# Partial sums of two token blocks kept in HBM between groups, in a chain of retention, gated MLP and MLP

## The chip, the cores and the metric

The kernel runs on one core of one Trainium2 chip. The metric is the device time of one execution in microseconds (us); a time given for the kernel is the median of several executions. A profile comes from one further execution. Engines are named as the profile names them: PE (TensorE's matmuls), PEld (its weight loads), DVE (VectorE), ACT (ScalarE), POOL (GpSimd), SP (SyncE, which issues most transfers).

## The reference, cut to what matters

```python
# q, k, v: (2, 8, 768, 64); 8 heads with decay gamma
for t in range(S):
    state = gamma * state + k_t (outer) v_t
    y[t] = scale * q_t @ state
x = y as (1536 tokens, 512)
# gated MLP, d_ff 1536
xn = x / sqrt(mean(x*x) + 1e-6) * rms_g
x = (silu(xn @ w_gate) * (xn @ w_val)) @ w_out
# MLP, d_ff 2048
h = x @ w_in
out = maximum(0.01 * h, h) @ w_out2
```

Inputs and outputs are 32-bit floats. This document is about the two output products, `@ w_out` (layer 1, called `o` in the code) and `@ w_out2` (layer 2, `p`), and about where their partial sums over d_ff are kept.

## The kernel before

**Tiling.** The 1536 tokens are three blocks of 512 (b = 0, 1, 2). d_ff is cut into slices f of 128: 12 in layer 1, 16 in layer 2. Four slices make a group: gi = 0, 1, 2 belong to layer 1 and gi = 3, 4, 5, 6 to layer 2. The weights come as 64-bit numbers; per slice ScalarE (`prepare`, L537 and L538, tiles `wa` and `wb`) and VectorE make 32-bit numbers of the loaded `raw` tile, and then split them into a high and a low part (`w_...`, H on ScalarE, L on VectorE). A product of two split operands is three matmuls of 512 columns.

**Seven products.** Blocks 1 and 2 go through a scheme with seven products of halves in place of eight (`quad` for the products into the hidden layer, `seventh` for the output products of groups 1, 3, 4, 5 and 6). In `seventh` the products run in the order 1, 2, 5, 6, 3, 7, 4, with twelve matmuls each in a group (two pairs of slices, two banks, three terms). Products 1, 6, 7 and 4 add up in the two PSUM banks `X`, products 2, 5 and 3 in two banks `Z`. After each product but the first the two banks are, as they then stand, the contribution of this group to one half of one block: 2 to block 1 row 0, 5 and 7 to block 2 row 1, 6 and 3 to block 2 row 0, 4 to block 1 row 1. So twelve banks are read out per group. Product 7 goes on adding into the banks that product 6 left, and product 4 into those that product 7 left. The order of the products with whole blocks between them stands in `plan`: one block of twelve matmuls follows products 1, 2, 6 and 4.

**Where the sums live.** Block 1's and block 2's sums are two SBUF tiles of 128 x 4 x 512 (`x2acc` in layer 1, `y2acc` in layer 2, both in the places `acc1` and `acc2`). In group 0 ScalarE copies the banks there (`evac1`, L673). Later VectorE adds each bank to its part of the tile: in groups 1 and 3 to 6 in `seventh` (L817; the first contribution of a half in group 3 is a ScalarE copy, L815), in group 2 in `evac1` (L675). Block 0 has long been treated otherwise: ScalarE copies its banks to the tile `more`, and GpSimd's transfers write or add them to HBM (`held`, L695 to L698, in layer 1; the rows of `out`, L851 and L853, in layer 2).

**Queues.** Each engine executes in the order of its own queue. What stands in that order comes from the program's order (the string `ORDER` for the head of the program, `plan` and the rules of `run` with its costs for the rest) and from the framework's scheduler, which may move instructions of one engine past each other. Read-outs are put into `later` with the letter of their engine, "a" or "v", and come out with `flush` behind the step. `gh` and `gl` are pools of three buffers for the split hidden values (`gq_4h`, `gp_0h` and so on).

Of the kernel before, what the change touches and what calls it, by code (L numbers as in the profile page):

```python
# [8 lines left out]
F32 = mybir.dt.float32  # L9
# [7 lines left out]
P = 128  # L17
# [46 lines left out]
def chain_kernel(ctx: ExitStack, tc: tile.TileContext, qk_t, kv, w1, w2, mask, qdec, kdec, sdec, rms_g, ident, out):  # L64
# [26 lines left out]
    sm = attn_pools.enter_context(tc.tile_pool(name="sm", bufs=4))  # L91

    held = [dram.tile([P, 512], F32, name=f"held{i}") for i in range(4)]
    mask_sb = const.tile([P, 2, NPAIR, CH], F32, name="mask_sb")
    qdec_sb = const.tile([P, NPAIR, CH], F32, name="qdec_sb")
    kdecs = const.tile([P, CPB - 1, 2 * NPAIR, 1], F32, name="kdecs")
# [500 lines left out]
    def accumulate(L, g, f, b, start, stop, transposed):  # L597

        if start:
            acc["b"] = acc_banks(f"a{L}_{g}_{b}", 4)  # L600
        h, l = parted.pop((L, f, b))
        w = wt[f"{L}{f}"]
        for m in range(4):
            part = slice(m * P, (m + 1) * P)
            if transposed:
                terms = (w[:, 0, part], h), (w[:, 0, part], l), (w[:, 1, part], h)
            else:
                terms = (h[:, part], w[:, 0, :]), (h[:, part], w[:, 1, :]), (l[:, part], w[:, 0, :])
            cut = 256 if stop and m == 3 and g == len(groups) - 1 else 512
            for c in range(0, 512, cut):  # L610
                for n, (lhs, rhs) in enumerate(terms):
                    nc.tensor.matmul(  # L612
                        out=acc["b"][m][:, c:c + cut],
                        lhsT=lhs,
                        rhs=rhs[:, c:c + cut],
                        start=(start and n == 0),
                        stop=(stop and n == 2),
                        skip_group_check=True,
                    )
# [45 lines left out]
    def evac1(gi, b, banks):  # L665
        last = gi == len(G1) - 1
        if b:
            if gi == 0:
                acc[b] = xp.tile([P, 4, 512], F32, tag=f"acc{b}", name=f"x2acc{b}")
            for m in range(4):  # L670
                dst = acc[b][:, m, :]
                if gi == 0:
                    nc.scalar.activation(out=dst, in_=banks[m], func=AF.Copy)  # L673
                else:
                    nc.vector.tensor_tensor(out=dst, in0=banks[m], in1=dst, op=ALU.add)  # L675
            if not last:
                return
            highs, lows = ([lambda m=m, do=do: do(m) for m in range(2 * b - 2, 4)] for do in x2_parts(b))
            if b == 1:
                sums.extend(highs + lows)  # L680
                return
            one, two = slice(0, 2), slice(2, 4)
            ops = sums_of(acc, x2h, x2l, acc[1][:, one], acc[1][:, two], x2h[2][:, one], x2l[2][:, one], extra()[:, two])
            both = [lambda i=i: [ops[n]() for n in (f"{i}", f"h{i}")] for i in range(4)]
            sums.extend(both[:2] + [ops["l1"]] + highs + [ops["l0"]] + lows + [both[2], ops["l2"], both[3], ops["l3"]])
            return
        acc[0] = extra()
        for m in range(4):
            t = acc[0][:, m, :]
            if last:  # L690
                nc.vector.tensor_tensor(out=t, in0=banks[m], in1=t, op=ALU.add)
                continue
            nc.scalar.activation(out=t, in_=banks[m], func=AF.Copy)
            if gi == 0:
                nc.gpsimd.dma_start(out=held[m], in_=t)  # L695
            else:
                nc.gpsimd.dma_start(out=held[m], in_=t, accum_op=ALU.add)
                nc.gpsimd.dma_start(out=t, in_=held[m])  # L698
        if last:
            high, low = x2_parts(0)  # L700
            sums.extend([lambda m=m, do=do: do(m) for do in (high, low) for m in range(4)])

    def x2_parts(b):
        if b not in x2h:
# [27 lines left out]

    AS = {"o": "r", "p": "q"}
    turns = {}
    touched = set()

    def follow(q, f, n):
        t = turns[q, f]
# [17 lines left out]
    def seventh(gi, n, f):  # L756
        fs = groups[gi][1]
        L = groups[gi][0][-1]
        key = (AS[L], f, n)
        if n == 1 and f == fs[0]:  # L760
            gather(gi)
        if n == 5 and f == fs[0] and gi == len(groups) - 1:
            recall()
        upper(key)
        lower(key)
        h, l = parted.pop(key)
        unit, half, side, start, (b, row) = SIDES[n]
        names = f"{L}{f}", f"{L}{f + 1}", f"s{L}{f}", f"s{L}{f + 1}"
        w = wt[names[unit]]
        if f == fs[0] and start:  # L770
            acc[side] = [acc_bank(i + 2 * (side == "Z"), f"{side}{gi}_{n}_{i}") for i in range(2)]
        for m in range(2):
            part = slice((2 * half + m) * P, (2 * half + m + 1) * P)
            wh, wl = w[:, 0, part], w[:, 1, part]
            for k, (lhs, rhs) in enumerate(((wh, h), (wh, l), (wl, h))):
                nc.tensor.matmul(  # L776
                    out=acc[side][m],
                    lhsT=lhs,
                    rhs=rhs,
                    start=(start and f == fs[0] and k == 0),  # L780
                    stop=(f == fs[-2] and k == 2),
                    skip_group_check=True,
                )
        if n == 1:
            used(names[0])
        elif n == 4:
            used(names[1])
        elif n in (7, 3):
            free(names[unit])
        placed[0] = order.index(key) + 1  # L790
        if f != fs[-2]:
            return
        if n == 1:
            acc["Z"] = seeded = [acc_bank(i + 2, f"Z{gi}_2_{i}") for i in range(2)]
            source = acc["X"]

            def seed():
                for m in range(2):
                    nc.scalar.activation(out=seeded[m], in_=source[m], func=AF.Copy)

            later.append(("a", 1.2, seed))
            return
        banks = acc[side]
        total = y2 if L == "p" else acc
        fresh = gi == len(G1) and (b, row) not in touched
        if L == "p":
            touched.add((b, row))
        if b not in total:
            y2[b] = xp.tile([P, 4, 512], F32, tag=f"acc{b}", name=f"y2acc{b}")

        def put():
            for m in range(2):
                dst = total[b][:, 2 * row + m, :]
                if fresh:
                    nc.scalar.activation(out=dst, in_=banks[m], func=AF.Copy)  # L815
                else:
                    nc.vector.tensor_tensor(out=dst, in0=banks[m], in1=dst, op=ALU.add)  # L817
            if gi == len(groups) - 1 and LAST[b, row] == n:
                t = units.tile([P, 2, 16, 32], F32, tag="u", name=f"turned{b}_{row}")
                for m in range(2):  # L820
                    nc.vector.transpose(
                        out=t[:, m], in_=y2[b][:, 2 * row + m, :].rearrange("p (j r) -> p j r", r=32)
                    )
                    for i in range(4):
                        o = (2 * row + m) * P + i * 32
                        nc.sync.dma_start(
                            out=out[offs[b]:offs[b] + 512, o:o + 32].rearrange("(j r) d -> r j d", r=32),
                            in_=t[32 * i:32 * i + 32, m],
                        )

        later.append(("a" if fresh else "v", 1.2, put))

    def evac2(gi, b, banks):
        first, last = gi == len(G1), gi == len(groups) - 1
        if first and b:
            y2[b] = xp.tile([P, 4, 512], F32, tag=f"acc{b}", name=f"y2acc{b}")
        for m in range(4):
            dst = y2[b][:, m, :] if b else more[0][:, m, :]
            rows = out[offs[b] + m * P:offs[b] + (m + 1) * P, :]
            if b and not first:  # L840
                nc.vector.tensor_tensor(out=dst, in0=banks[m], in1=dst, op=ALU.add)
            elif last:
                cut = 256 if m == 3 else 512
                for c in range(0, 512, cut):
                    part = partial[m][:, c:c + cut]
# [1 line left out]
                    nc.sync.dma_start(out=rows[:, c:c + cut], in_=part)  # L847
            else:
                nc.scalar.activation(out=dst, in_=banks[m], func=AF.Copy)
                if not b and first:  # L850
                    nc.gpsimd.dma_start(out=rows, in_=dst)  # L851
                elif not b:
                    nc.gpsimd.dma_start(out=rows, in_=dst, accum_op=ALU.add)  # L853

    more = {}
# [135 lines left out]
    def quad(n, f):  # L991
# [27 lines left out]
            later.append(("v" if n == "v" else "a", 0.6, lambda: use[n](key, src, place(n, key))))  # L1019

        def p1():
            q["X"] = bank(f"{n}X{f}")
            half(q["X"], own[0], False, "B11", True)
            if seeded:
# [344 lines left out]
```

## Time and profile before

| what | value |
|---|---|
| median of 3 executions | 581.53 us (581.23 to 582.47) |
| the profiled execution | 581.64 us |
| its span in the profile | 579.9 us |
| PE, DVE, ACT, POOL busy | 570.6, 503.7, 366.9, 38.9 us |
| moved by all transfers | 60.13 MB |

The span runs from the first to the last thing that the profile records; 1.7 us of the profiled execution lie around it. Busy time of PE is from a matmul's start to its modelled end, and matmuls overlap, so a full PE row does not by itself say that no time is lost: starts that lie further apart than usual do. `L612` and the like are lines of the kernel before.

### The profile page before, as it was taken

To read this page: it belongs to the slowest core of one execution; us is meant where nothing else is said; L and a number is where in the kernel's file an instruction comes from. 1 tells how busy PE (TensorE), PEld (TensorE's weight loads), DVE (VectorE), ACT (ScalarE), POOL (GpSimd) and SP (SyncE) were. 2 spreads that over 40 slices of the span, in tenths; PEclk is the share of its full clock that TensorE was granted. 3 is DMA by queue.
4 is the path that set the end of the run, shared out by engine and by line. 5 is a ranking of instruction groups with operands and counts; after the bars stand their busy time and mean duration, and the time that the engine had idled before them with its cause. 6 is when DMAs were issued, how large, how long until landed. Compare 5 with 4: busy or idle time off the path is not lost.

```text
span 579.9 us, 8491 instructions
## 1 busy us (share of the span) xinstructions
PE 570.6 (98%) x3098; PEld 469.9 (81%) x3098; DVE 503.7 (87%) x924; ACT 366.9 (63%) x676; POOL 38.9 (7%) x48
## 2 busy tenths in 40 slices
PE   8899999999999999999999999999999999999997
PEld 5788788888888888887888878888888888888886
DVE  5899999997676899997579999999899979995783
ACT  2789656776556465674564568877856876675430
POOL 2332100010000000030000000000100020002100
PEclk9999999999999999999999999999999999999999
DMA  8991240444012211382410111123420453011725
GB/s 326 408 392 62 73 145 1 146 147 144 6 68 74 72 38 36 111 224 105 141 61 14 37 36 37 44 103 109 148 70 7 139 116 103 1 37 22 160 50 133
DMA packets 34922, 60.13 MB, mean 104 GB/s; under 512 B 19392, under 2 KB 19776, under 8 KB 34880
## 3 DMA queue, kind: packets, MB, share of 16 engines
q1 hardware_dynamic: 31728, 52.24, 27.2%
q0 software_dynamic: 3008, 7.34, 5.4%
q8 instruction: 24, 0.39, 0.3%
q14 instruction: 18, 0.15, 0.1%
q10 hardware_dynamic: 144, 0.00, 0.0%
HBM read 51.19 MB, written 8.39 MB: 103 GB/s over the span
## 4 chain that ended last, share of the span: by engine, by line
PE 80%; DMA 7%; DVE 7%; ACT 4%; issue 1%; POOL 0%; DVEq 0%; ACTq 0%; SPq 0%; POOLq 0%
PE ao L612 11%; PE X L776 9%; PE iX L984 8%; PE ap L612 8%; PE i L581 8%; PE Z L776 7%; PE v L581 6%; PE g L581 5%; PE vX L984 4%; PE iZ L984 4%; PE gX L984 4%; PE vZ L984 2%; PE gZ L984 2%; PE iY L984 2%; DMA qkv<-in_qk_t 2%; DMA qkv<-in_kv 2%
## 5 line engine op out<-in xcount | busy, mean ns | idle before, releaser
L612 PE MATMUL ap<-w_p,gp_0h 128*128 128x512 f32 (+1 forms) x130 | 40.2, 386 | 0.0
L581 PE MATMUL i<-x2h,w_i 128*128 128x512 f32 x128 | 32.0, 389 | 0.0
L581 PE MATMUL v<-xh,w_v 128*128 128x512 f32 x128 | 31.9, 390 | 0.0
L581 PE MATMUL g<-xh,w_g 128*128 128x512 f32 x128 | 31.8, 391 | 0.0
L612 PE MATMUL ao<-go_0h,w_o 128*128 128x512 f32 x96 | 31.7, 389 | 0.0
L612 PEld LDWEIGHTS ap<-w_p,gp_0h 128*128 128x128 f32 x130 | 24.4, 188 | 5.0
L581 PEld LDWEIGHTS g<-xh,w_g 128*128 128x128 f32 x128 | 24.0, 188 | 5.1 <-issue 0.2
L581 PEld LDWEIGHTS i<-x2h,w_i 128*128 128x128 f32 x128 | 24.0, 188 | 5.0
L581 PEld LDWEIGHTS v<-xh,w_v 128*128 128x128 f32 x128 | 24.0, 188 | 4.9
L612 PE MATMUL ap<-w_p,gp_0l 128*128 128x512 f32 (+1 forms) x65 | 25.1, 386 | 0.0
L612 PEld LDWEIGHTS ao<-go_0h,w_o 128*128 128x128 f32 x96 | 18.0, 188 | 3.7
L612 PE MATMUL ao<-go_2h,w_o 128*128 128x512 f32 x64 | 20.6, 391 | 0.1
L612 PE MATMUL ao<-go_1h,w_o 128*128 128x512 f32 x64 | 20.4, 389 | 0.0
L984 PE MATMUL iZ<-x2h,w_si 128*128 128x512 f32 x64 | 20.4, 392 | 0.0
L984 PE MATMUL iX<-th,w_si 128*128 128x512 f32 x64 | 19.9, 392 | 0.0
L922 ACT ACTIVATE more<-i 128x512 f32<-128x512 f32 x16 | 9.5, 596 | 15.8 <-PE i L581 15.7
L538 ACT ACTIVATE wb_i<-raw_i 128x512 int32<-128x512 uint32 x16 | 10.7, 670 | 13.6 <-DMA raw_i<-in_w 4.0
L612 PE MATMUL ao<-go_0l,w_o 128*128 128x512 f32 x48 | 18.7, 389 | 0.0
L627 ACT ACTIVATE gp_0h<-more 128x512 fp32r<-128x512 f32 x16 | 10.1, 631 | 11.9 <-PE X L776 5.8
L581 PE MATMUL v<-xl,w_v 128*128 128x512 f32 x64 | 17.2, 391 | 0.0
L581 PE MATMUL g<-xl,w_g 128*128 128x512 f32 x64 | 17.2, 391 | 0.0
L581 PE MATMUL i<-x2l,w_i 128*128 128x512 f32 x64 | 17.1, 389 | 0.0
(382 smaller groups left out, 1770.0 us busy)
## 6 DMA issues: line engine op xcount, KB each, us to landing
raw_i<-in_w SPq DMA_DIRECT2D x16, 512.0 KB, 3.6
raw_p<-in_w SPq DMA_DIRECT2D x16, 512.0 KB, 3.5
raw_g<-in_w SPq DMA_DIRECT2D x12, 512.0 KB, 3.5
raw_v<-in_w SPq DMA_DIRECT2D x12, 512.0 KB, 3.6
raw_o<-in_w SPq DMA_DIRECT2D x12, 512.0 KB, 3.6
qkT<-in_qk_t SPq DMA_DIRECT2D x7, 512.0 KB, 7.1
kv<-in_kv SPq DMA_DIRECT2D x7, 512.0 KB, 8.5
out<-more POOLq DMA_DIRECT2D x12, 256.0 KB, 4.4
```

The costliest lines, as they stand in the source:

```text
L538: nc.scalar.activation(out=m, in_=low.bitcast(U32), func=AF.Copy, scale=2.0 ** -29)
L581: nc.tensor.matmul(out=dst, lhsT=lhs, rhs=rhs, start=(n == 0), stop=(n == len(pairs) - 1), skip_group_check=True)
L612: nc.tensor.matmul(out=acc["b"][m][:, c:c + cut], lhsT=lhs, rhs=rhs[:, c:c + cut], start=(start and n == 0), stop=(stop and n == 2), skip_ ...
L627: nc.scalar.activation(out=h, in_=x, func=AF.Copy)
L776: nc.tensor.matmul(out=acc[side][m], lhsT=lhs, rhs=rhs, start=(start and f == fs[0] and k == 0), stop=(f == fs[-2] and k == 2), skip_group ...
L922: nc.scalar.activation(out=a, in_=x, func=AF.Prelu, alpha=0.01)
L984: nc.tensor.matmul(out=dst, lhsT=lhs, rhs=rhs, start=(start and n == 0), stop=(n == 5), skip_group_check=True)
```

## The change

Blocks 1 and 2 are treated much as block 0 was. Eight HBM tiles per layer, `summed`, hold the sums of the two blocks. Outside the last group of a layer, `put_away` copies each bank with ScalarE to one of eight places of two SBUF tiles (`awayo`, `awayp`, in the same places `acc1` and `acc2`), which are used in turn, and GpSimd issues a transfer from there to the HBM tile: a plain one the first time, an adding one afterwards. Before the last group's sums are due, `bring` reads the eight tiles back (`osum`, `psum`), and VectorE adds the last group's banks to them as before. Layer 1's reads are issued as block b's output product of group 2 begins, layer 2's at the second `quad` of group 6.

```diff
     held = [dram.tile([P, 512], F32, name=f"held{i}") for i in range(4)]
+    summed = {(L, b): [dram.tile([P, 512], F32, name=f"sum{L}{b}{m}") for m in range(4)] for L in "op" for b in (1, 2)}
...
             acc["b"] = acc_banks(f"a{L}_{g}_{b}", 4)
+            if b and g == len(G1) - 1:
+                bring("o", b)
...
     def evac1(gi, b, banks):
         last = gi == len(G1) - 1
         if b:
-            if gi == 0:
-                acc[b] = xp.tile([P, 4, 512], F32, tag=f"acc{b}", name=f"x2acc{b}")
             for m in range(4):
-                dst = acc[b][:, m, :]
-                if gi == 0:
-                    nc.scalar.activation(out=dst, in_=banks[m], func=AF.Copy)
+                if last:
+                    dst = acc[b][:, m, :]
+                    nc.vector.tensor_tensor(out=dst, in0=banks[m], in1=dst, op=ALU.add)
                 else:
-                    nc.vector.tensor_tensor(out=dst, in0=banks[m], in1=dst, op=ALU.add)
+                    put_away("o", b, m, banks[m])
...
+    begun = set()
+    places = {}
+    turn_at = [0]
+
+    def put_away(L, b, m, src):
+        if (L, "at") not in places:
+            places[L, "at"] = [xp.tile([P, 4, 512], F32, tag=f"acc{i}", name=f"away{L}{i}") for i in (1, 2)]
+        t = places[L, "at"][turn_at[0] // 4 % 2][:, turn_at[0] % 4, :]
+        turn_at[0] += 1
+        nc.scalar.activation(out=t, in_=src, func=AF.Copy)
+        if (L, b, m) in begun:
+            nc.gpsimd.dma_start(out=summed[L, b][m], in_=t, accum_op=ALU.add)
+        else:
+            begun.add((L, b, m))
+            nc.gpsimd.dma_start(out=summed[L, b][m], in_=t)
+
+    def bring(L, b):
+        into = acc if L == "o" else y2
+        into[b] = xp.tile([P, 4, 512], F32, tag=f"acc{b}", name=f"{L}sum{b}")
+        for m in range(4):
+            nc.gpsimd.dma_start(out=into[b][:, m, :], in_=summed[L, b][m])
...
-        fresh = gi == len(G1) and (b, row) not in touched
...
+        final = gi == len(groups) - 1
 
         def put():
             for m in range(2):
-                dst = total[b][:, 2 * row + m, :]
-                if fresh:
-                    nc.scalar.activation(out=dst, in_=banks[m], func=AF.Copy)
+                if final:
+                    dst = y2[b][:, 2 * row + m, :]
+                    nc.vector.tensor_tensor(out=dst, in0=banks[m], in1=dst, op=ALU.add)
                 else:
-                    nc.vector.tensor_tensor(out=dst, in0=banks[m], in1=dst, op=ALU.add)
+                    put_away(L, b, 2 * row + m, banks[m])
...
-        later.append(("a" if fresh else "v", 1.2, put))
+        later.append(("v" if final else "a", 1.2, put))
...
         def p1():
+            if f == groups[-1][1][-2]:
+                for b in (1, 2):
+                    bring("p", b)
```

`evac2` loses its branches for blocks 1 and 2, which no longer come there.

**ScalarE, group 4, about product 7.** Names ending in h are high parts of hidden values, `w_si` and `w_i` high parts of weights, `wa_p` a weight's first step. Before:

```order
L627 ACTIVATE gq_7h<-iu_6_3968 128x512
L428 ACTIVATE w_si_4352<-wa_i_4088 128x512
L537 ACTIVATE wa_p_4430<-raw_p_4348 128x512
L627 ACTIVATE gq_4h<-i_1_3825 128x512
L487 ACTIVATE w_i_4362<-wa_i_4333 128x512
L627 ACTIVATE gq_4h<-i_1_3955 128x512
L487 ACTIVATE w_i_4421<-wa_i_4365 128x512
L537 ACTIVATE wa_p_4495<-raw_p_4395 128x512
```

After:

```order
L630 ACTIVATE gq_7h<-iu_6_4026 128x512
L429 ACTIVATE w_si_4422<-wa_i_4146 128x512
L713 ACTIVATE awayp_3655<-Z_5_0_4234 128x512
L713 ACTIVATE awayp_3655<-Z_5_1_4235 128x512
L630 ACTIVATE gq_4h<-i_1_3883 128x512
L488 ACTIVATE w_i_4432<-wa_i_4404 128x512
L630 ACTIVATE gq_4h<-i_1_4013 128x512
L713 ACTIVATE awayp_3654<-X_1_0_4111 128x512
L538 ACTIVATE wa_p_4500<-raw_p_4418 128x512
L713 ACTIVATE awayp_3654<-X_1_1_4112 128x512
```

The copies of product 3's banks (`Z_5`) now stand between `w_si` and the first `gq_4h`, where one `wa_p` stood; the copies of product 7's banks (`X_1`) come behind the second `gq_4h`, with a `wa_p` between them.

**PE, group 4, from product 7 to product 4.** `i_0` is a whole block of other work. Before:

```order
L776 MATMUL X_1_1_4054<-gq_7h,w_sp_4110 128x512
L581 MATMUL i_0_4318<-x2h_3078,w_i_3861 128x512 x5
L776 MATMUL X_1_0_4053<-gq_4h,w_p_3983 128x512
L776 MATMUL X_1_0_4053<-gq_4l,w_p_3983 128x512
L776 MATMUL X_1_0_4053<-gq_4h,w_p_3983 128x512
L776 MATMUL X_1_1_4054<-gq_4h,w_p_3983 128x512
```

After:

```order
L798 MATMUL X_1_1_4112<-gq_7h,w_sp_4168 128x512
L582 MATMUL i_0_4388<-x2h_3114,w_i_3919 128x512
L798 MATMUL X_1_0_4111<-gq_4h,w_p_4041 128x512
L798 MATMUL X_1_0_4111<-gq_4l,w_p_4041 128x512
L798 MATMUL X_1_0_4111<-gq_4h,w_p_4041 128x512
L798 MATMUL X_1_0_4111<-gq_4h,w_p_4143 128x512
L798 MATMUL X_1_0_4111<-gq_4l,w_p_4143 128x512
L798 MATMUL X_1_1_4112<-gq_4h,w_p_4041 128x512
```

One filler is left of five, and five of the six matmuls on the first bank now stand ahead of the first on the second bank. The groups 1, 3 and 5 had four, two and six fillers and have one each.

**POOL, at the end of group 5.** Nothing stood here before but the transfers of block 0. After:

```order
L715 DMA sump_110<-awayp_3654 128x512
L715 DMA sump_111<-awayp_3655 128x512
L724 DMA psum_5122<-sump_105 128x512
L715 DMA sump_112<-awayp_3655 128x512
L724 DMA psum_5122<-sump_106 128x512
L715 DMA sump_107<-awayp_3655 128x512
L715 DMA sump_108<-awayp_3655 128x512
L724 DMA psum_5122<-sump_107 128x512
```

A read back of block 1's sums (`psum`) stands ahead of the last adding transfers of group 5 (`sump_112`, `sump_107`, `sump_108`).

## Rows read from the trace of the kernel before

**Rows 1.** The page, busy us by engine (share of the span) and instructions.

```profile
PE 570.6 (98%) x3098; PEld 469.9 (81%) x3098; DVE 503.7 (87%) x924; ACT 366.9 (63%) x676; POOL 38.9 (7%) x48
```

**Rows 2.** Waits of PE; us in total, times, longest. The only one after 67 us.

```profile
PE vX L984 <- ACT vu L1004: 0.3, 1, 0.3
```

**Rows 3.** The chain of waits; start us, us, what. Pieces of twelve matmuls.

```profile
382.89 2.87 PE X L776 x12
...
426.10 2.72 PE Z L776 x12
...
501.15 2.75 PE X L776 x12
```

**Rows 4.** Windows; stretch, length, busy us of PE, PEld, DVE, ACT, POOL; clock, DMA.

```profile
416.00:443.00 27.00, 27.00 (x120) 22.10 (x119) 25.86 (x46) 17.42 (x31) 0.00 (x0) 1.00 0.16 55
```

**Rows 5.** Timeline of PE; start us, us, instruction. Group 4, product 7 to 4.

```profile
439.54 1.29 PE L581 MATMUL i<-x2h,w_i 128*128 128x512 f32 x5
440.83 0.47 PE L776 MATMUL X<-gq_4h,w_p 128*128 128x512 f32 x1
441.14 0.39 PE L776 MATMUL X<-gq_4l,w_p 128*128 128x512 f32 x1
```

**Rows 6.** Timeline of PE, the same place in group 1.

```profile
225.68 1.07 PE L581 MATMUL v<-xh,w_v 128*128 128x512 f32 x4
...
226.93 0.40 PE L776 MATMUL X<-gr_4l,w_o 128*128 128x512 f32 x1
```

**Rows 7.** Timeline, chain of waits and DMA issues about 265 and 324 us.

```profile
raw_i<-in_w SPq DMA_DIRECT2D x16, 512.0 KB, 3.6
...
256.79 6.62 DMA raw_i<-in_w
...
263.51 0.66 ACT L538 ACTIVATE wb_i<-raw_i 128x512 int32<-128x512 uint32 x1 [2.09 <-DMA raw_i<-in_w]
265.12 0.58 ACT L1004 ACTIVATE vu<-vX 128x512 f32<-128x512 f32 x1
...
264.34 1.07 PE L581 MATMUL g<-xl,w_g 128*128 128x512 f32 x4
266.31 0.40 PE L984 MATMUL vX<-tl,w_sv 128*128 128x512 f32 x1
...
324.13 0.39 PE L612 MATMUL ao<-go_1h,w_o 128*128 128x512 f32 x1
324.95 0.39 PE L612 MATMUL ao<-go_2l,w_o 128*128 128x512 f32 x1
```

**Rows 8.** Timeline of DVE in group 4.

```profile
440.00 1.28 DVE L817 TENSOR_TENSOR y2acc<-X,y2acc 128x512 f32<-128x512 f32 x2
441.20 0.68 DVE L635 TENSOR_TENSOR gp_0l<-more,gp_0h 128x512 fp32r<-128x512 f32 x1
```

**Rows 9.** Timeline of ACT in group 3, two copies and what follows.

```profile
374.11 1.07 ACT L815 ACTIVATE y2acc<-X 128x512 f32<-128x512 f32 x2
375.06 0.64 ACT L627 ACTIVATE gq_7h<-iu 128x512 fp32r<-128x512 f32 x1
```

**Rows 10.** Timeline of ACT in group 4.

```profile
436.78 0.66 ACT L537 ACTIVATE wa_p<-raw_p 128x512 f32<-128x512 f32 x1
437.34 0.62 ACT L627 ACTIVATE gq_4h<-i 128x512 fp32r<-128x512 f32 x1
...
438.39 0.62 ACT L627 ACTIVATE gq_4h<-i 128x512 fp32r<-128x512 f32 x1
438.92 0.62 ACT L487 ACTIVATE w_i<-wa_i 128x512 fp32r<-128x512 f32 x1
```

**Rows 11.** Instructions by line: adding transfers (issue, landing; min/median/max), the last adds.

```profile
L697 POOL DMA_DIRECT2D held<-more x4: 875/1078/1297, 249.7 to 252.2; - x4
...
DMA to landing us min/median/max: 4.9/6.2/8.3
...
L817 DVE TENSOR_TENSOR y2acc<-Z,y2acc x6: 682/684/685, 543.3 to 557.5; 128x512 f32<-128x512 f32 x6
```

More of the change, by code (lines that the diff above doesn't have):

```diff
@@ L734, in chain_kernel @@
     turns = {}
-    touched = set()
     def follow(q, f, n):
@@ L803, in seventh @@
         banks = acc[side]
-        total = y2 if L == "p" else acc
-        fresh = gi == len(G1) and (b, row) not in touched
[L806 to L809, printed above, removed]
+        final = gi == len(groups) - 1
         def put():
             for m in range(2):
-                dst = total[b][:, 2 * row + m, :]
-                if fresh:
-                    nc.scalar.activation(out=dst, in_=banks[m], func=AF.Copy)
+                if final:
+                    dst = y2[b][:, 2 * row + m, :]
+                    nc.vector.tensor_tensor(out=dst, in0=banks[m], in1=dst, op=ALU.add)
                 else:
-                    nc.vector.tensor_tensor(out=dst, in0=banks[m], in1=dst, op=ALU.add)
+                    put_away(L, b, 2 * row + m, banks[m])
             if gi == len(groups) - 1 and LAST[b, row] == n:
@@ L829, in put @@
                         )
-        later.append(("a" if fresh else "v", 1.2, put))
+        later.append(("v" if final else "a", 1.2, put))
     def evac2(gi, b, banks):
+        assert not b
         first, last = gi == len(G1), gi == len(groups) - 1
-        if first and b:
-            y2[b] = xp.tile([P, 4, 512], F32, tag=f"acc{b}", name=f"y2acc{b}")
         for m in range(4):
-            dst = y2[b][:, m, :] if b else more[0][:, m, :]
+            dst = more[0][:, m, :]
             rows = out[offs[b] + m * P:offs[b] + (m + 1) * P, :]
-            if b and not first:
-                nc.vector.tensor_tensor(out=dst, in0=banks[m], in1=dst, op=ALU.add)
-            elif last:
+            if last:
                 cut = 256 if m == 3 else 512
@@ L849, in evac2 @@
                 nc.scalar.activation(out=dst, in_=banks[m], func=AF.Copy)
-                if not b and first:
+                if first:
                     nc.gpsimd.dma_start(out=rows, in_=dst)
-                elif not b:
+                else:
                     nc.gpsimd.dma_start(out=rows, in_=dst, accum_op=ALU.add)
```

## The prediction

> **What bounds the kernel now.** I read the page first: matmuls fill 570.6 of 579.9 us, VectorE 503.7, ScalarE 366.9, GpSimd 38.9 [rows 1]. That alone does not say whether TensorE sets the pace or merely looks full, so I went to the waits, and then to the timeline. From 67 us on TensorE shows one wait, 0.3 us [rows 2]. In the chain of waits twelve matmuls of 512 columns take 2.72 us, 0.227 us each [rows 3], and that cadence is my ruler: what a stretch takes beyond its count times 0.227 is lost. VectorE is nearly full in the stretches where the changed work lies (25.9 of 27 us), ScalarE has a third of them free (17.4 of 27) [rows 4]. So VectorE is busy but not late. The time to be won is what TensorE loses, and the time to be paid is any new loss there.
>
> Where it loses now. In four groups (gi = 1, 3, 4, 5) the seven products of a group run in the order 1, 2, 5, 6, 3, 7, 4. Product 4 adds into the banks that product 7 has just left, so it must wait until those have been read out; the scheduler slips matmuls of other work between. In group 4, product 4's second matmul stands 1.60 us behind the first of five such fillers, which six at 0.227 (1.36) would fill: 0.24 lost [rows 5]. By the same count, group 1 loses 1.25 - 5 x 0.227 = 0.12 [rows 6]; groups 3 and 5 show it as pieces of 2.87 and 2.75 instead of 2.72, 0.15 and 0.03 [rows 3]. Together 0.54 us. Two larger losses lie elsewhere: 1.97 - 1.36 = 0.61 us at 265 us, and 0.82 - 0.45 = 0.37 us at 324 us [rows 7].
>
> **The change, part by part.**
>
> *Adds leave VectorE.* 40 adds of one bank go (12 each in groups 1, 4, 5, and 4 in group 3; the 8 adds that end layer 1 and the 12 of the last group stay). Two of them begin at 440.00 and the next instruction at 441.20, 0.60 us each [rows 8], so VectorE is relieved of 40 x 0.60 = 24 us. No matmul waits for VectorE over that stretch, so this pays only where a wait named above ends in it: nothing by itself.
>
> *Copies come to ScalarE.* The same 40 banks are copied by ScalarE; two such copies of group 3 start 0.475 us apart and the second ends 0.60 after its start [rows 9]. That is 40 x 0.475 = 19 us more, in group 4 some 12 x 0.6 = 7.2 busy us on top of 17.4, 24.6 of 27. In sum it fits; the question is the one place where TensorE waits at once, product 7 to 4. There VectorE used to read the banks, now ScalarE does, in its own queue. Take group 4. Today ScalarE starts the second gq_4h at 438.39 and its next instruction 0.53 later [rows 10]. In the new order one wa_p that stood ahead (0.56 us, 436.78 to 437.34 [rows 10]) is gone from there and the two copies of Z_5 stand in its place (2 x 0.475). So gq_4h starts at 438.39 - 0.56 + 0.95 = 438.78, the copy of X_1_0 at 439.31, ready at 439.91. (The bank itself is done earlier: its last matmul starts four ahead of 439.54, at 438.63.) From a ScalarE end to the matmul that waited for it: vu ends at 265.70, and the second matmul behind at 266.31 puts the first at 265.86 [rows 7], 0.16 us. So TensorE could go on at 440.07. It has one filler instead of five and stands ready at 439.54 + 0.23 = 439.77: **0.30 us lost**. The second bank is not late again: X_1_1's copy starts after one more wa_p (439.31 + 0.53 + 0.56 = 440.40, ready 441.0, seen 441.16), and five matmuls on X_1_0 stand before it (440.07 + 1.13 = 441.20). The margin is 0.04, no more. In groups 1, 3, 5 the same number of ScalarE instructions stands between gq_7h (gr_7h) and that copy; I take 0.30 for each, so 4 x 0.30 = 1.2 in place of 0.54: **+0.7 us**. Bounds: at the low end the copy lands on time, -0.54; at the high end ScalarE is one more instruction in arrears each time (0.53), 4 x 0.83 - 0.54 = +2.8. I take the row-by-row value.
>
> *Other banks.* The copies after products 2, 5, 6 and 3 have 2.72 us of other work or more before their bank is written again, against two copies of 1.08 us together; nothing. What else stands behind them on ScalarE (splits h, the Y copy of the next block) comes up to 1 us later; the Y copy has product 4, the rest of a full block and seven more matmuls ahead of it. Cost nothing, cover under 1 us in group 3, where ScalarE was fullest.
>
> *Transfers come to GpSimd.* 72 in all: 16 plain writes, 40 accumulating, 16 reads back. Accumulating ones take GpSimd 1.08 us to issue at the median and land after 4.9 to 8.3 us [rows 11]; 72 at that price, the plain ones' bound from above, are 78 us on an engine that is busy for 39 of 580. A slot is written again eight copies later. The tightest pair is product 5 to product 4: filled after 428.8, wanted again near 443 [rows 3, 5], 14 us, against two issues and a landing, 2 x 1.08 + 8.3 = 10.5. Nothing, with over 3 us to spare. GpSimd's queue is in order, and a read back stands ahead of the last adds of group 5; what waits behind it is wanted 40 us later: the last group's first add is at 543.3 [rows 11], group 5 ends at 503.9 [rows 3]. Layer 1's sums of group 1 leave some 5 us after 227 and are wanted back at 324 [rows 6, 7]. Nothing either way. Block 0's own transfers stand behind them, by tens of us.
>
> *Ends.* The head (67 us) and the tail behind the last matmul are not touched.
>
> **Sum.** The profiled execution took 581.64 us, 0.11 above the median of 581.53. 581.64 + 0.7 = 582.3 on its footing, 582.2 on the median's. A difference under 0.2% (1.16 us) can't be told from none.
>
> **The rivals.**
>
> *A. Weight loads get in the way of ScalarE (slower).* At 265 us one weight load took 6.62 us, while its kind lands in 3.6 at the median; GpSimd's transfers for block 0 were in flight. ScalarE stood 2.09 us before wb_i for it, and TensorE then lost 0.61 [rows 7]. The change puts twelve more such transfers into each of the four groups. The Trainium skill states the rule behind this in "DMA: Bandwidth & Descriptors", section "Issuing engines are not separate DMA queues": transfers share the same 16 DMA engines and interleave, whichever engine started them; that 6.62 us load agrees. Against it: three weights are loaded ahead, and the waits of ScalarE for loads were rare. One such stall per group adds 4 x 0.61 = 2.4: 584.6. It decides from one stall in all, which puts the sum over +1.16.
>
> *B. ScalarE becomes the bound (slower).* The high end above, +2.8: 584.3. For it: about 91% of the stretch is filled. Against: every instruction in front of the copy was placed by its row.
>
> *C. VectorE was the bound (faster).* It is nearly full [rows 4], and all weight splits pass through it. The most that can come back is what TensorE loses: 0.54 + 0.61 + 0.37 = 1.5: 580.0. Against: the loss at 265 began with a load, the one at 324 with adds that stay. The Trainium skill, "Perfetto Trace Analysis", section "Identifying the Most-Contended Engine", would judge TensorE by weight-loading time and not by matmul time, since pipelined matmuls mislead. By it 81% are used, VectorE with 87% is the fullest engine, and 24 us could come back, 557. The row of twelve matmuls in 2.72 us without a gap speaks against that reading, and its chance is a small part of C's.
>
> *D. A copy waits for its slot*, because accumulations on one tile queue up: beyond 14 us from copy to landing ScalarE stands and all behind it. It takes over 3 us beyond the slowest landing shown. Each us of it, four times, is 4 us: 586.
>
> **How the numbers follow.** Forecast 0.60 (its own range 581.4 to 583.0; of it 0.50 within 0.2%, 0.10 slower), A 0.14, B 0.13, D 0.03, C 0.10 (0.06 faster, 0.04 the same). So faster 0.06, same 0.54, slower 0.40. The range runs from 580.9 (copies on time, -0.54, with a little of C) to 584.4 (B whole); C's far end, part of A and D lie outside.
>
> **What would show it.** Right: VectorE 24 to 28 us less busy, ScalarE about 24 more; product 4's first matmul behind ScalarE's L713 with a few tenths lost in each of four groups; no wait of L713 for a transfer; the losses at 265 and 324 still there. Wrong: new gaps of half a us in front of blocks whose weights came late (A), gaps that grow through a group (B), L713 idle for a transfer (D), or the four gaps closed and the one at 265 gone (C).

## The result, and the profile after

The changed kernel takes 589.5 us at the median of four executions (588.97 to 591.41), the kernel before 581.38 beside it on the same chip; ratio 1.0143, 95% interval 1.0116 to 1.017. It is slower by 8 us, outside the range that the prediction gave. The profiled execution has a span of 587.45 us against 579.87, **7.58 more**.

The page of the changed kernel: engines, two DMA queues, two kinds of weight load (median us to landing).

```profile
PE 572.1 (97%) x3098; PEld 469.2 (80%) x3098; DVE 482.5 (82%) x884; ACT 384.5 (65%) x716; POOL 92.3 (16%) x120
...
q1 hardware_dynamic: 31728, 52.24, 27.4%
q0 software_dynamic: 11328, 26.22, 21.7%
...
raw_i<-in_w SPq DMA_DIRECT2D x16, 512.0 KB, 4.2
...
raw_v<-in_w SPq DMA_DIRECT2D x12, 512.0 KB, 4.9
```

The page of the kernel before had, for GpSimd's queue:

```profile
q0 software_dynamic: 3008, 7.34, 5.4%
```

Against [rows 1] VectorE is 21.2 us less busy, ScalarE 17.6 more, GpSimd 53.4 more, as the change says. The new thing stands in the last lines: GpSimd's transfers now fill 21.7% of the sixteen DMA engines' time in place of 5.4%, and a raw_i load lands after 4.2 us in place of 3.6 [rows 7].

Where TensorE loses: the prediction's ruler (0.227 us a matmul), applied to every start from 67 us on that is over 0.02 us late, gives 2.27 us lost before and 9.95 after. That is 7.68 more, as much as the whole difference. (A wait of 0.27 us for GpSimd at 69 us, which [rows 2] leaves out, is in both kernels.) The loss lies in two kinds of place. The first is the crossing from product 7 to product 4; the timeline of PE in group 4 (start us, us, what):

```profile
445.00 0.39 PE L582 MATMUL i<-x2h,w_i 128*128 128x512 f32 x1
445.34 0.50 PE L798 MATMUL X<-gq_4h,w_p 128*128 128x512 f32 x1
445.67 0.39 PE L798 MATMUL X<-gq_4l,w_p 128*128 128x512 f32 x1
```

Two steps take 0.67 where 0.45 would do: 0.22 lost. Groups 1, 3 and 5 lose 0.22, 0.28 and 0.22, in all 0.95 in place of 0.54. The second kind is new. The waits of PE (us in total, times, longest):

```profile
PE iY L998 <- ACT iY L1043: 3.2, 2, 1.7
PE vX L998 <- ACT vu L1018: 1.7, 1, 1.7
...
PE gX L998 <- ACT gu L1018: 1.3, 1, 1.3
```

From start to start, less 0.227 a step, these are 1.62 us at 244 us and 0.41 at 252 (both `gX`, behind group 1), 1.97 at 267 (`vX`; 0.61 before [rows 7]), 1.93 at 406 and 1.86 at 468 (`iY`, behind groups 3 and 4): 7.18 more than before, and with 0.41 from the crossings 7.59 of the 7.58. The chain of waits shows what stands in front of them: here pieces of it ahead of the stops at 244, 267, 406 and 468.

```profile
235.33 0.63 ACT wa_g L538
235.96 6.23 DMA raw_v<-in_w
...
242.27 0.66 ACT wa_v L538
242.94 0.57 ACT wb_v L539
...
259.39 7.40 DMA raw_i<-in_w
...
393.04 5.76 DMA raw_i<-in_w
...
447.64 8.35 DMA raw_p<-in_w
...
457.78 0.70 DVE wa_p L476
...
458.53 4.07 DMA raw_i<-in_w
```

ScalarE in its timeline (start us, us, what, and how long it stood idle before it and for what):

```profile
242.27 0.66 ACT L538 ACTIVATE wa_v<-raw_v 128x512 f32<-128x512 f32 x1 [3.31 <-DMA raw_v<-in_w]
...
245.02 0.67 ACT L539 ACTIVATE wb_v<-raw_v 128x512 int32<-128x512 uint32 x1 [0.99 <-DVE wa_g L485]
245.59 0.58 ACT L1018 ACTIVATE gu<-gX 128x512 f32<-128x512 f32 x1
...
398.90 0.66 ACT L539 ACTIVATE wb_i<-raw_i 128x512 int32<-128x512 uint32 x1 [3.34 <-DMA raw_i<-in_w]
```

The pieces that begin with DMA are weight loads: of 6.23 us ahead of the stop at 244, 7.40 ahead of 267, 5.76 ahead of 406, 8.35 and 4.07 ahead of 468. ScalarE, in order, stands at wa or wb until its load has landed, and what TensorE wants next (`gu` at L1018, the copy `iY` at L1043) comes behind it in its queue. The next load cannot start meanwhile, since VectorE frees a raw buffer only after ScalarE's step: at 457.78 its step on `raw_p` (L476), and behind it, at 458.53, the load of `raw_i`. So lateness is handed on from load to load. The DMA engines in the stretch before the stop at 244 (windows; the last two numbers are their busy share and GB/s):

```profile
224.00:244.00 20.00, 20.00 (x88) 16.26 (x87) 16.45 (x33) 14.50 (x27) 9.57 (x14) 1.00 0.98 233
```

They are full: 0.98. (The share adds up the time of all packets that begin in the stretch, so it can come out a little over 1.) In the kernel before the same stretch had 0.20. No copy of L713 waited for its place, at any time.

### The profile page after: what moved, and what is told of

It is laid out like the page before. It is cut to its first block, busy times and chain, and to the rows that moved or that the text cites. A ratio compares the mean times of both kernels' runs of the same rounds, so it can differ in the third digit from the quotient of the medians.

```text
span 587.5 us, 8668 instructions
## 1 busy us (share of the span) xinstructions
PE 572.1 (97%) x3098; PEld 469.2 (80%) x3098; DVE 482.5 (82%) x884; ACT 384.5 (65%) x716; POOL 92.3 (16%) x120
## 3 DMA queue, kind: packets, MB, share of 16 engines
q0 software_dynamic: 11328, 26.22, 21.7%
## 4 chain that ended last, share of the span: by engine, by line
PE 72%; DMA 12%; ACT 8%; DVE 6%; issue 1%; SPq 0%; POOL 0%; DVEq 0%; ACTq 0%; POOLq 0%
PE ao L615 11%; PE X L798 8%; PE i L582 7%; PE Z L798 6%; PE v L582 6%; PE ap L615 5%; PE g L582 5%; PE iX L998 5%; PE vX L998 4%; PE gX L998 4%; DMA raw_i<-in_w 3%; PE iZ L998 2%; PE vZ L998 2%; DMA qkv<-in_qk_t 2%; PE gZ L998 2%; DMA qkv<-in_kv 2%
## 5 line engine op out<-in xcount | busy, mean ns | idle before, releaser
L715 POOL DMA_DIRECT2D sump<-awayp x28 | 24.8, 941 | 40.8 <-ACT awayp L713 26.4
L718 POOL DMA_DIRECT2D sump<-awayp x8 | 4.5, 572 | 114.0 <-ACT awayp L713 114.0
L715 POOL DMA_DIRECT2D sumo<-awayo x12 | 10.9, 978 | 47.1 <-ACT awayo L713 46.8
```

The source lines that it names most:

```text
L715: nc.gpsimd.dma_start(out=summed[L, b][m], in_=t, accum_op=ALU.add)
L718: nc.gpsimd.dma_start(out=summed[L, b][m], in_=t)
```

## The experiments

Theory 1: GpSimd's transfers crowd the weight loads on the DMA engines, loads come late, and ScalarE's order passes that on to TensorE. Theory 2: the new order and the 40 more copies on ScalarE hold the weight steps back, whatever is moved.

**The transfers thinned.**

```diff
-            nc.gpsimd.dma_start(out=summed[L, b][m], in_=t, accum_op=ALU.add)
+            nc.gpsimd.dma_start(out=summed[L, b][m][:1], in_=t[:1], accum_op=ALU.add)
```

(the plain write likewise; `bring` reads `held`).

> The change with each of its 56 writes to memory cut to one of 128 partition rows; its 40 copies by ScalarE, its places and the order of every engine stay, and the reads back at the end take other data, so the sums of two blocks are left out. Theory 1 (the transfers crowd the weight loads): the five large gaps of the changed kernel go or fall to the 0.6 us of before, and of the 7.7 us that TensorE lost more only the crossings' 0.4 stays: 581.5 to 582.6. Theory 2 (the new order and ScalarE's copies hold the weight steps back, whatever the transfers move): nothing comes back, 588.5 to 590. Half of each: about 585.5.

Measured: 581.58 us, ratio 1.0003 (0.9994 to 1.0013). The whole loss is gone with every engine's order and all 40 copies in place. Its page and its timeline of PE where the changed kernel stopped at 244:

```profile
q0 software_dynamic: 6080, 11.66, 8.9%
```

```profile
244.42 0.39 PE L615 MATMUL ao<-go_0h,w_o 128*128 128x512 f32 x1
244.64 0.62 PE L998 MATMUL gX<-th,w_sg 128*128 128x512 f32 x2
```

Theory 2 falls. It also shows that 21 us less work on VectorE bring no gain that can be told from none, and that the crossings (0.96 us here, 0.54 before) cost 0.4, no more than the prediction's 0.7. One warning: ScalarE waits 10.4 us for raw_i loads in this run, nearly as long as in the changed kernel (12.0). Waits of an engine that has slack are no loss; only what TensorE then waits for counts. The two raw_i loads ahead of 267 show it best. In the thin variant:

```profile
L395 SPq DMA_DIRECT2D raw_i<-in_w x2: 327/328/328, 254.8 to 256.4; - x2
...
DMA to landing us min/median/max: 7.7/8.0/8.3
```

The first takes 7.7 us, longer than its 7.40 in the changed kernel, and ScalarE stands 4.9 us for it. Yet TensorE loses nothing here, for it was issued at 254.8; in the changed kernel it was issued at 259.39, held up by the late loads in front of it. What counts is when a load lands, not how long it takes.

**Accumulating or plain.**

```diff
-            nc.gpsimd.dma_start(out=summed[L, b][m], in_=t, accum_op=ALU.add)
+            nc.gpsimd.dma_start(out=summed[L, b][m], in_=t)
```

> The change with the 40 accumulating transfers made plain writes of the same size, so that each tile keeps only its last group's part (the sums of two blocks are left out). Theory 1 with bytes alone: as many bytes are written, the gaps stay, 588 to 590. Theory 1 with the accumulation itself as the cost (each such transfer reads the tile in memory too): loads return half way, gaps fall to half, 584 to 586.5. Theory 2: 588.5 to 590.

Measured: 582.46 us, ratio 1.0021 (1.0011 to 1.0032), below every range expected: a miss, in the direction of the reading by accumulation (584 to 586.5). The same 72 transfers and bytes cost 0.9 us more than thin ones; adding in memory makes the rest, some 7 us. The page of the profile says why:

```profile
q0 software_dynamic: 8768, 26.22, 14.4%
```

The same 26.22 MB fill 14.4% in place of 21.7%. In time of all sixteen engines: 14.4% of 580.1 us is 83.5, less the 31.3 of before (5.4% of 579.9) leaves 52.2 for 72 transfers, **0.73 us a plain one** (writes and reads back together). 21.7% of 587.5 is 127.5, 44.0 more for the 40 that accumulate, 1.1 on top of 0.73: **1.8 us each**. The rows also show how: 11328 packets against 8768 for the same bytes, 64 more for each of the 40, where a plain transfer has 64 (of 4 KB). The twelve of a group are 22 us in a stretch of 27.

**Is it occupancy?** Three plain writes (3 x 0.73) for one accumulating (1.8).

```diff
-            nc.gpsimd.dma_start(out=summed[L, b][m], in_=t, accum_op=ALU.add)
+            nc.gpsimd.dma_start(out=summed[L, b][m], in_=t)
+            for k in range(2):
+                nc.gpsimd.dma_start(out=spare[L, b, k][m], in_=t)
```

> The change with each of its 40 accumulating transfers replaced by three plain writes of the same place, to three tiles of their own (sums of two blocks left out). By the queue shares of the earlier runs a plain write takes 11.6 us of one DMA engine's time, an accumulating one 29.2, so three plain ones (34.8) fill the engines more than the accumulating one did. If occupancy of the DMA engines is what delays the weight loads: 588 to 593. If it is something that only accumulating transfers do to the packets beside them: 582 to 584.

Measured: 595.82 us, ratio 1.0228 (1.0197 to 1.0259), above the 588 to 593 that occupancy had forecast and far from the rival's 582 to 584.

```profile
q0 software_dynamic: 15168, 47.20, 23.8%
```

So it is what the transfers take of the engines, not the adding as such. Time and packets aren't told apart by this: the packets of this queue rise in the same order as the loss (6080, 8768, 11328 and 15168 from thin to tripled). The changed kernel, the thin, the plain and the tripled one have the same order on TensorE, VectorE and ScalarE, and in all of them the same two raw_v loads of group 2 are issued at 236.0 and 237.5 (within 0.2), so they can be laid side by side. The tile's own lines, for the changed kernel, the plain, the thin and the tripled one:

```profile
L395 SPq DMA_DIRECT2D raw_v<-in_w x2: 327/328/328, 236.0 to 237.5; - x2
...
DMA to landing us min/median/max: 5.9/6.1/6.2
```

```profile
L395 SPq DMA_DIRECT2D raw_v<-in_w x2: 328/328/328, 235.9 to 237.4; - x2
...
DMA to landing us min/median/max: 4.3/5.2/6.0
```

```profile
L395 SPq DMA_DIRECT2D raw_v<-in_w x2: 327/328/328, 235.8 to 237.4; - x2
...
DMA to landing us min/median/max: 3.4/3.8/4.1
```

```profile
L396 SPq DMA_DIRECT2D raw_v<-in_w x2: 328/328/328, 236.0 to 237.6; - x2
...
DMA to landing us min/median/max: 7.4/7.7/8.1
```

| kernel | DMA share, 224 to 244 us | the two loads, median us | lost at 244 us | time, us |
|---|---|---|---|---|
| thin | 0.41 | 3.8 | 0 | 581.58 |
| plain | 0.77 | 5.2 | 0.2 | 582.46 |
| the change | 0.98 | 6.1 | 1.6 | 589.5 |
| tripled | 1.00 | 7.7 | 2.8 | 595.82 |

Each row is worse than the one above it in every column.

**The copies on VectorE.**

```diff
-        nc.scalar.activation(out=t, in_=src, func=AF.Copy)
+        nc.vector.tensor_copy(out=t, in_=src)
```

> The change with its 56 copies done by VectorE in place of ScalarE; the transfers stay as they are. ScalarE has the load of before less the first copies, VectorE 33 us more than in the change. Theory 1: the loads are as slow as in the change, and ScalarE still stands before wb and wa: 587.5 to 590. Theory 2: ScalarE is relieved, weight steps come in time: 581 to 583.

Measured: 588.01 us, ratio 1.0121 (1.0094 to 1.0149), as theory 1 has it. TensorE still stands 1.8 us at `vX` and 1.7 at `iX`, for ScalarE's steps that came behind late loads (7.01 us ahead of `vX`, 6.86 ahead of `iX`).

**The transfers in the kernel before.** Adds stay on VectorE; the tile is sent after each.

```diff
                     nc.vector.tensor_tensor(out=dst, in0=banks[m], in1=dst, op=ALU.add)
+                if gi < len(groups) - 1:
+                    send(L, b, 2 * row + m, dst)
```

> The kernel before with the transfers alone: VectorE adds as before, and after each of the 56 bank read-outs GpSimd sends the tile to memory, plain the first time and accumulating afterwards, to tiles that nobody reads. The order of TensorE, VectorE and ScalarE is that of before. Theory 1: medians of the weight loads rise from 3.5 to over 4 us, TensorE gets gaps of 1 to 2 us after groups 1, 3 and 4, in all 4 to 7 us: 585.5 to 588.5. Theory 2: nothing waits for these transfers, 581.0 to 582.0.

Measured: 591.51 us, ratio 1.017 (1.0119 to 1.0221), more than expected, and for another reason. VectorE in its timeline, at the crossing of group 1:

```profile
227.21 0.69 DVE L829 TENSOR_TENSOR x2acc<-Z,x2acc 128x512 f32<-128x512 f32 x1 [2.82 <-DMA sumo<-x2acc]
```

The add of product 3 waits for a transfer that is still reading the tile since product 6; product 4 then waits 3.4 us for VectorE. That wait was put in by the experiment, so it decides nothing. The same without it (products 5 and 6 send nothing, 7 and 3 twice):

> As the run with the transfers alone in the kernel before, with one flaw taken out: there a tile was sent after products 5 and 6 and added to again by 7 and 3 some 8 us later, so an add could wait for a transfer to have read its tile. Now 5 and 6 send nothing and 7 and 3 send twice: the same 16 plain and 40 accumulating transfers, all adds on VectorE, the order of TensorE, VectorE and ScalarE that of before. Theory 1 (accumulating transfers crowd the weight loads, in any order): no matmul waits for an add, the loads take over 4 us, gaps of 1 to 2 us behind weight blocks, 584.5 to 588.5. Rival (they crowd the loads, but only the changed kernel's order has too little slack to bear it): 581.2 to 582.5.

Measured: 587.94 us, ratio 1.0117 (1.0092 to 1.0143). The order of the kernel before doesn't protect it: transfers alone cost 6.6 us, with stops of the same kind. The waits of PE in the profiled execution, the fastest of the four (586.35):

```profile
PE iY L998 <- ACT iY L1040: 1.9, 2, 1.5
...
PE vX L998 <- ACT vu L1018: 1.2, 1, 1.2
```

**Only layer 1's made plain.** The accumulation is kept for `L == "p"` alone.

> The change with the 12 accumulating transfers of group 1 made plain (block 1's and 2's sums of group 0 are left out in layer 1), those of layer 2 accumulate as in the change. Theory 1, by place: the gaps at 244, 252 and 267 us go (1.62 + 0.41 + 1.86 less what plain writes left, 0.2), those behind groups 3 and 4 stay: 585.5 to 586.3. If the loss moves on to the next place instead of going: 588 to 590.

Measured: 586.25 us, ratio 1.0084 (1.007 to 1.0098). In time it is as expected: it lies 3.2 us below the change and 3.8 above the plain variant (586.25 - 582.46). In place it is a miss. The stop at 244 shrank to 0.3 and the one at 252 went, but the one at 267 stayed (2.06), and of the two that were to stay, the one behind group 4 shrank from 1.86 to 0.35, though its transfers are those of the change. So the range was hit by other stops than forecast, which is luck, and 3.2 and 3.8 are differences between medians, not prices of a group's transfers. Up to 267 the program is that of the plain variant, whose trace loses only 0.1 at this place. So a stop depends on how transfers and loads happen to meet in an execution, and one profile's gap shouldn't be put down to an edit.

**Fewer transfers.** The banks of products 7 and 3 are added by VectorE into the place of 5 and 6, and only the sum is sent.

```diff
+                elif n in (6, 5):
+                    waiting[b, row, m] = t = spot(L)
+                    nc.scalar.activation(out=t, in_=banks[m], func=AF.Copy)
+                elif n in (3, 7):
+                    t = waiting.pop((b, row, m))
+                    nc.vector.tensor_tensor(out=t, in0=banks[m], in1=t, op=ALU.add)
+                    ship(L, b, 2 * row + m, t)
```

> The change with fewer transfers: the banks of products 5 and 6 are copied to their places as before, those of 7 and 3 are added there by VectorE, and only then is each place sent: 24 accumulating and 16 plain writes in place of 40 and 16, none accumulating in group 3. If the cost goes by their number: 8 us x 24/40 on top of 581.5, 586.3. If it goes by what overlaps within a group (a load is late only when several run beside it): the gap behind group 3 (1.9 us) goes entirely and the others shrink to under half, 582.5 to 584.5. If the order alone mattered: 588.5 to 590.

Measured: 588.13 us, ratio 1.0114 (1.0084 to 1.0144): a miss, 40% fewer accumulations bought 1.4 us, which the spread of the executions hides. The stop behind group 3 did go, but one of 2.9 us came at 244 and one of 1.7 at 517. Two controls in this variant's order, its writes plain, and its writes thin:

> The variant with 24 accumulating transfers, with these made plain; the order of all engines is that variant's own. If its 588.1 us came from its 24 accumulating transfers: 581.5 to 583. If it came from its other order of products and weight steps: 586.5 to 589.

> The variant with adds of products 7 and 3 in their places, its 40 writes cut to one of 128 partition rows each, the reads back taking other data; the order of all engines is that variant's own. If its loss (588.1, and 589.4 with plain writes) is its order's, whatever is moved: 587.5 to 590. If in that order even plain writes crowd the loads enough: 581.3 to 583.

Measured: 589.37 (1.0102 to 1.0141) and 583.42 (1.0021 to 1.0044), both outside the ranges given for them. The first can't be read as a price of plain writes. Its profiled execution, the slowest of the four (591.44), came late out of the head. One instruction of TensorE's, with the writes accumulating and with the writes plain:

```profile
68.69 0.66 PE L311 MATMUL norm<-ident_sb,nr 128*64 128x128 f32 x8 [0.27 <-POOL nr L305]
```

```profile
75.10 0.66 PE L311 MATMUL norm<-ident_sb,nr 128*64 128x128 f32 x8 [0.27 <-POOL nr L305]
```

That is 6.4 us, lost before the first of the 56 writes is issued (141 and 147 us). From there on the plain variant takes 3.3 us less than the accumulating one. What the head took in its other executions isn't known. Nor are the thin variant's 1.8 us shown to be its order's. It keeps the sixteen reads back at full size, and in its profiled execution, again the slowest (586.24), TensorE stands 2.8 us before 515.7 behind a weight load that was issued among them:

```profile
504.65 5.72 POOL L733 DMA_DIRECT2D psum<-held  x8
...
507.27 7.16 DMA raw_p<-in_w
```

So in this order too most of the loss is gone with the bytes (588.13 to 583.42). How much of it accumulation makes, and why this order bears so little, stays open.

**Block 0's transfers, in the kernel before and in the changed one.** In group 1 the accumulate into memory and the read back become one transfer that adds into SBUF:

```diff
-                nc.gpsimd.dma_start(out=held[m], in_=t, accum_op=ALU.add)
-                nc.gpsimd.dma_start(out=t, in_=held[m])
+                nc.gpsimd.dma_start(out=t, in_=held[m], accum_op=ALU.add)
```

> The kernel before with block 0's four pairs in group 1 (accumulate into memory, read back) made one each: the tile in SBUF is the target and the sum in memory is added to it by the transfer. Theory 1: fewer and earlier transfers beside the weight loads, the 0.6 us at 265 us goes, 580.7 to 581.1. If that gap has another cause: 581.3 to 581.6.

Measured in the kernel before: **580.80 us**, ratio 0.9989 (0.998 to 0.9998), 0.56 us less. Its timeline of PE:

```profile
264.11 1.07 PE L581 MATMUL g<-xl,w_g 128*128 128x512 f32 x4
265.01 0.62 PE L983 MATMUL vX<-th,w_sv 128*128 128x512 f32 x2
265.47 0.39 PE L983 MATMUL vX<-tl,w_sv 128*128 128x512 f32 x1
```

Six matmuls in 1.36 us: the 0.61 of [rows 7] is gone. This is faster than both kernels, by little.

> The change with block 0's four pairs (accumulate into memory, read back) in group 1 made one transfer each, as in the variant of the kernel before that ran in 580.8. The gap at 267 us (1.86 in the changed kernel) follows a weight load of 7.4 us beside those transfers. If that gap is theirs: 1 to 2 us less than the change, 587.5 to 588.5. If the loss only moves on: 589 to 590.

Measured in the changed kernel: 590.32 us, ratio 1.0151 (1.013 to 1.0172), a miss, just above the range for a loss that moves on. The stop at 267 went, but the one at 244 grew from 1.7 to 2.8 us from start to start: the loss moved.

## Why the prediction was wrong, point by point

- **What bounds the kernel**: right. TensorE sets the pace and VectorE's 24 us (21.2 came) were worth nothing that can be told from none; the thin variant has VectorE relieved and stands at 1.0003 (0.9994 to 1.0013). So rival C is out, and with it the reading by weight-loading time.
- **The crossing from 7 to 4**: right in mechanism. PE's product 4 stands behind L713, in each of four groups. 0.30 each was predicted, 0.22, 0.28, 0.22 and 0.22 came: +0.4 in place of +0.7, less by 0.02 to 0.08 a group.
- **Slots and ScalarE's load** (rivals D and B): right to be small. No copy waited for its place, and with all copies but thin transfers nothing is lost. (The prediction has two figures for ScalarE, 19 us more where it is worked out and 24 in the signs; 17.6 came.)
- **The step that failed** is the last sentences of *Transfers come to GpSimd*: "Nothing either way". The term was worked out for GpSimd's issue (1.08 us) and the landing of a slot, that is, for the transfers' own users. What they take from the weight loads on the sixteen DMA engines stood only in rival A, and there at a price copied from one row: 0.61 us a stop, 2.4 in all. The runs put 7.9 us there: 0.9 for thin transfers made full plain ones (581.58 to 582.46) and 7.0 for 40 of them made accumulating (to 589.5), in the profile four stops of 1.6 to 2.0 us and a smaller one. Rival A had the mechanism right and its size wrong: a late load also holds up the next one, as ahead of 267 and 468, which a price copied from a single stop leaves out. The chance of 0.14 rested on "the waits of ScalarE for loads were rare", which was so at the DMA share of 0.16 of [rows 4] and says nothing about 0.70, which the same stretch of group 4 has now:

```profile
420.00:447.00 27.00, 27.00 (x120) 22.09 (x119) 21.71 (x40) 22.66 (x43) 9.27 (x12) 1.00 0.70 138
```

- **What the profile of before would have told.** Its queue row above is 31.3 us of all sixteen engines for 28 transfers (16 plain, 12 accumulating), 1.1 us each. Twelve more in 27 us are 13 us at that mean, half the stretch, on top of 0.16; with the 1.8 us found above for accumulating ones it is the stretch's greater part, and where they come close together the engines are full. And the kernel before had its twelve accumulating transfers in three fours. The first, from 249.7, met weight loads: 244 to 264 us had a DMA share of 0.87 and the one long load and stop [rows 7]. Around the other two, from 472.8 and from 532.7, one weight load was issued (3.6 us to landing) and TensorE lost nothing. The row was read as an exception; it was the one sample of such transfers among several loads.
- **The pages.** The rule cited with rival A, in the Trainium skill's "DMA: Bandwidth & Descriptors", section "Issuing engines are not separate DMA queues", that transfers of all issuing engines share the 16 DMA engines and interleave, holds here: two loads from SyncE's queue landed after 3.8 us beside thin transfers from GpSimd and after 7.7 beside the tripled ones. The same page of the Trainium skill gives, under "Anatomy of one DMA — SWDGE (gpsimd) path", a fit of 2.0 us and the bytes over 436 GB/s for one transfer from GpSimd, an estimate of 2.6 us for 256 KB. In the plain variant layer 1's twenty writes landed after 2.8 at the median; with twelve of them accumulating, as in the change, after 5.0, in a stretch whose DMA engines are full; the fit doesn't cover that.

## What to carry to other kernels

A transfer that nobody waits for is not free: price it as time on the shared DMA engines (share of the queue row times span, divided by its count), and compare with what is idle in that stretch, not in the whole span. Such a sum tells where loads will be late, not what a transfer costs: with 16 of 40 accumulations taken out only 1.4 of 8 us came back. An accumulating transfer into memory took 2.5 times the engine time of a plain one here. Where loads are only three buffers ahead and an in-order engine stands at the head of each, a load that takes 2 to 5 us longer than its kind can become a stop of 1.5 to 2 us of TensorE, and taking work off an engine that nobody waits for doesn't pay for that.

## What was not expected of the hardware

A long stop of TensorE can cost more than itself. In the changed kernel with block 0's single transfers, TensorE stood from 244.63 to 247.42; the windows around it (length, PE busy, granted clock, DMA share, GB/s):

```profile
240.00:244.80 4.80, 4.80 (x23) 1.00 0.77 287
244.80:247.40 2.60, 0.22 (x1) 0.99 0.94 280
247.40:250.00 2.60, 2.58 (x6) 0.50 0.98 317
```

After it the granted clock is 0.50, the lower of the two levels (1.2 GHz), for 2.6 us with 6 matmuls in place of 11. After the stops of 1.7 to 2.1 us from start to start in the changed kernel the clock stayed at 1.00. The length of the stop alone doesn't decide, though: the tripled variant stood a little longer at the same place, from 244.54 to 247.42, and went on at full clock, with 11 matmuls in 2.6 us:

```profile
247.40:250.00 2.60, 2.58 (x11) 1.00 1.01 350
```

What else decides isn't shown here. Where the clock falls, the loss is larger than the stop; that is part of why the tripled variant (a stop of 3.8 us at 471.55, then 427 ns a matmul) is so slow. Executions also spread more with the transfers in: 588.97 to 591.41 for the change and 580.98 to 582.47 for the kernel before.
